# Two one-block passes in place of one two-block pass at the end of a first layer

## The chip, the core and the metric

The kernel runs on one core of one Trainium2 chip. The metric is the device time of one execution in microseconds (us). Its engines are named as in the profile: PE is TensorE's matmuls and PEld its weight loads, DVE is VectorE, ACT is ScalarE, POOL is GpSimd, SP is SyncE, whose queue issues the DMAs.

## The reference

Two branches read the same rows x (2048 rows of 512) and are mixed by a gate per row.

```python
g = sigmoid((x * gate_w).sum(-1, keepdims=True))

# a: attention over all 2048 rows, 32 heads of 16
q, k, v = split_heads(x @ wqkv)
p = softmax(q @ k.T * 16 ** -0.5)
a = merge_heads(p @ v) @ wo

# b: a token mixer, F = 1792
h = (x - mean) / sqrt(var + 1e-5)              # per row
u = einsum("bsd,sf->bdf", h, w1) + b1          # (1, 512, 1792)
u = gelu(u)                                    # tanh form
y = einsum("bdf,fs->bds", u, w2) + b2
b = transpose(y)                               # (1, 2048, 512)

out = g * a + (1 - g) * b
```

## The kernel before

Every product keeps float32 precision with three matmuls: each operand is split into a high and a low part (`split`: a rounding copy, then a subtraction), and the products high-high, high-low and low-high add up in PSUM.

The stages that follow one another on TensorE are the values v, the projections of keys and queries (`project`, L75), the mixer's first layer (`layer`, L424), and then 128 attention phases in which the second layer's matmuls (L1076), the remaining query projections and the output projection run beside the scores (L1067), on the other half of the array's rows.

**The first layer.** The output u has 14 blocks of 128 columns of F. A pass makes up to four blocks at once (`NB` = 512 columns), each in a PSUM bank of its own (`bank`), and goes through the 16 row blocks c of h. There are passes of 4, 4, 4 and 2 blocks. For each c, `weight()` issues the load of a coming piece of w1 (`load_weight`, L146, on SyncE's queue), splits the piece that is next in line (`split_weight`: the cast w_hi on ScalarE at L67, the subtraction w_lo on GpSimd at L68) and gives out the oldest one that is split. There are four raw buffers and three each of w_hi and w_lo, so a split runs as soon as TensorE is done with the piece three before it. A piece is 128 rows by 512 columns, in the last pass 128 by 256. The first layer's last pass begins with row block 8 and ends with 7, so that the second half of h is free halfway through it; the memory of that half goes to attention's tiles (ot, the second query stack and others). `load_next` issues small loads of the first key and query stacks at every other c.

**The gelu** of a block is a generator of seven steps on two engines in turn: add the bias (VectorE, L433, which frees the PSUM bank), square (ScalarE, L435), the cubic factor times u (VectorE, L437 and L438), tanh (ScalarE, L440), outer product (VectorE, L442), high part (ScalarE, L444), low part (VectorE, L446). Its tiles gu and gs have two buffers each. The gelus of a pass run in the next pass. In passes 1 and 2 (counted from 0) the compiler's scheduler places them. In pass 3 the queues of ScalarE, VectorE and GpSimd follow the written order (`manual_schedule`), and the four gelus of pass 2 take a step per row block, beginning at row blocks 0, 1, 7 and 8:

```python
for i, step in enumerate(gelus):
    if 0 <= at - i // 2 * STEPS - i % 2 < STEPS:
        next(step)
```

**The late blocks.** The two blocks of the last pass have their gelus in the first attention phases: `late_u` adds the bias at once (L549), which frees their banks for scores; then `squares` (L555), `cubic` (L559), `inner` (L563), `tanh` (L566), `outer` (L570) and `outer_parts` (the two parts) are called at points of phases 0 to 3 given by `amid` (before the last two scores of a phase), `later` (after the phase's exps) and `on_dve`. All but the tanh run on VectorE. They work in `late_s`, one of two large tiles into which `load_xt` (L597) later brings a piece of transposed x.

**An attention phase** makes 16 score tiles. Ten of them get their exp on ScalarE straight from PSUM, six singly (L1093) and four as two pairs (L1031); six are copied out by VectorE (L1089) and get one long exp together (L1102). In attention all five engines follow the written order. The scores of a phase use seven banks in turn.

Of the kernel before, what the change touches and what calls it, by code (L numbers as in the profile page):

```python
# [13 lines left out]
AF = mybir.ActivationFunctionType  # L14
ALU = mybir.AluOpType
# [8 lines left out]
P = 128  # L24
S = 2048
D = 512
F = 1792
H = 32
DH = 16
NS = S // P  # L30
ND = D // P
NF = F // P
NB = 512
# [4 lines left out]
GELU_A = 0.044715  # L38
# [22 lines left out]
def gated_mix(ctx: ExitStack, tc: tile.TileContext, a_x, a_wqkv, a_wo, b_w1, b_b1, b_w2, b_b2, gate_w, out):  # L61
    nc = tc.nc
# [30 lines left out]
    g = const.tile([P, NS], F32, name="g")  # L93
# [29 lines left out]
    xt_lo = xt_pool.tile([P, ND, S], F32R, name="xt_lo")  # L123


    order = {f0: [(c + (NS // 2 if f0 + NB >= F else 0)) % NS for c in range(NS)] for f0 in range(0, F, NB)}
    blocks = [b_w1[c * P : (c + 1) * P, f0 : min(f0 + NB, F)] for f0 in order for c in order[f0]]
    blocks += [
        b_w2[c * P : min(c + 4, NF) * P, t * P : (t + 1) * P].rearrange("(k p) s -> p k s", p=P)
        for t in range(NS)  # L130
# [26 lines left out]
    def weight():  # L157
        load_weight()
        split_weight()
        return ready.pop(0)  # L160
# [17 lines left out]
    with tc.tile_pool(name="vp", bufs=1, side="right") as pool:  # L178
# [122 lines left out]
        for t in range(2, NS):  # L301
# [9 lines left out]
            ps = bank()  # L311
# [22 lines left out]
    h_hi, h_lo = {}, {}  # L334
# [28 lines left out]
    if True:  # L363
# [19 lines left out]
        for b in range(ND):  # L383
            wk_b, wq_b = qk_w.pop(0), qk_w.pop(0)
            kmax = bd.tile([P, NQ], F32, name="kmax")
            for at, (n, keys) in enumerate(jobs):
                ps = project(wk_b if keys else wq_b, n)
# [11 lines left out]
                if at in (2, 5):  # L399
                    c = 2 * b + at // 3  # L400
# [16 lines left out]
    u_hi = u_pool.tile([P, NF, D], F32R, name="u_hi")  # L417
    u_lo = u_pool.tile([P, NF, D], F32R, name="u_lo")

    def layer(ps, hi, lo, rhs, first, last):  # L420
        for i, p in list(enumerate(ps))[:: 1 if len(ps) == NB // P else -1]:
            wh, wl = hi[:, i * P : (i + 1) * P], lo[:, i * P : (i + 1) * P]
            for k, (a, b) in enumerate(((wh, rhs[0]), (wh, rhs[1]), (wl, rhs[0]))):
                nc.tensor.matmul(p, a, b, start=first and k == 0, stop=last and k == 2)  # L424

    with tc.tile_pool(name="gl", bufs=2, side="right") as gl:

        def gelu(ps, fb):

            u = gl.tile([P, D], F32, name="gu")  # L430
            s = gl.tile([P, D], F32, name="gs")
            hi, lo = u_hi[:, fb, :], u_lo[:, fb, :]
            nc.vector.tensor_scalar_add(u, ps, b1[:, fb : fb + 1])  # L433
            yield
            nc.scalar.activation(s, u, AF.Square)  # L435
            yield
            nc.vector.tensor_scalar(s, s, GELU_A, 1.0, ALU.mult, ALU.add)  # L437
            nc.vector.tensor_mul(s, s, u)  # L438
            yield
            nc.scalar.activation(s, s, AF.Tanh, scale=GELU_C)  # L440
            yield
            nc.vector.scalar_tensor_tensor(u, s, 1.0, u, ALU.add, ALU.mult)  # L442
            yield
            nc.scalar.copy(hi, u)  # L444
            yield
            nc.vector.tensor_tensor(lo, u, hi.bitcast(F32), ALU.subtract)  # L446
            yield

        beside = {mybir.EngineType.Activation, mybir.EngineType.DVE, mybir.EngineType.Pool}
        for c in range(AHEAD):  # L450
            ln_load(NH + c)


        def shift_rows(engine, t):
            for i in range(2):
                engine.memset(t[i * HALF + SHIFT[0] : i * HALF + SHIFT[0] + DH].bitcast(F32), -1.0)

        landed, waiting = [], []

        def stack(dst, src, which, pair, planes):  # L460
            b, r0 = divmod(pair * 2 * DH, P)
            for i in range(2):
                rows = slice(r0 + i * DH, r0 + (i + 1) * DH)
                for row, *part in planes:
                    at = slice(i * HALF + row, i * HALF + row + DH)
                    waiting.append((dst[at].bitcast(F32), src[b][part[which], rows, :]))

        def load_next():
            if waiting:
                landed.append(nc.sync.dma_start(*waiting.pop(0)))  # L470

        def load_all():
            while waiting:
                load_next()

        def load_k(g):
            t = k_bufs[g % 2]
            stack(t, kp_d, 1, g % NP, PAIRS)
            if g:
                load_all()  # L480
            return t

        def load_q(g):
            half, pair = divmod(g, NP)
            t = q_bufs[g % 2]
            stack(t, qp_d[half], 0, pair, [*PAIRS, SHIFT])
            if g:
                load_all()
            return t

        k_bufs, q_bufs = [], []

        def first_loads():
            k_bufs.append(first_stacks.tile([P, S], F32R, name="ks"))
            q_bufs.append(first_stacks.tile([P, QW], F32R, name="qs"))
            shift_rows(nc.vector, k_bufs[0])
            return {0: load_k(0)}, {0: load_q(0)}

        STEPS = 7
        gelus = []  # L500
        for f0, cs in order.items():
            n = min(NB, F - f0) // P
            ps = [bank() for _ in range(n)]
            in_order = f0 == 0 or f0 + NB >= F
            if f0 == NB:
                kt, qt = first_loads()
            if not in_order:
                for step in gelus:
                    list(step)
                gelus = []  # L510
            with tc.manual_schedule(engines=beside) if in_order else ExitStack():
                for at, c in enumerate(cs):
                    hi, lo = weight()

                    if f0 == 0 and AHEAD < c <= NH:
                        ln_load(NH + c - 1)
                    if f0 == 0 and AHEAD < c <= NH + AHEAD:
                        ln_rows(NH + c - AHEAD - 1)
                    layer(ps, hi, lo, (h_hi[c], h_lo[c]), at == 0, at == NS - 1)
                    if at % 2:  # L520
                        load_next()
                    for i, step in enumerate(gelus):
                        if 0 <= at - i // 2 * STEPS - i % 2 < STEPS:
                            next(step)
            gelus = [gelu(ps[i], f0 // P + i) for i in range(n)]
    h_ctx.close()


# [17 lines left out]
    for i, p in reversed(list(enumerate(ps))):  # L546
        u = out_pool.tile([P, D], F32, name="row", bufs=3)
        at = NF - len(ps) + i
# [136 lines left out]
    calls, later, amid = {}, {}, {}  # L685
# [4 lines left out]
    def on_dve(at, *what):  # L690
        later.setdefault(at, []).append(what)
# [161 lines left out]
            on_dve(2 * at + 2, *finish)  # L853
        return put(steps, at, [len(steps)])

    for i in range(2):
        on_dve(1 + i, tanh, i)
        on_dve(2 + i, outer_parts, i)
    for p, mid, what, i in (
        (0, True, squares, 0),  # L860
        (0, False, cubic, 0),
        (1, True, inner, 0),
        (1, False, squares, 1),
        (1, False, cubic, 1),
        (2, True, inner, 1),
        (2, False, outer, 0),
        (3, True, outer, 1),
    ):
        if mid:
            amid.setdefault(p, []).append((what, i))  # L870
        else:
            later.setdefault(p, []).insert(1 if what is cubic and i else 0, (what, i))
    call(3, load_xt, 2)
    for b in range(ND):
        call(6 + b, nc.sync.dma_start, v_d[b], vb[b][:, :BV])
    at, queries = 0, [(b, n) for n in (2, 3) for b in range(ND)]
    for t in range(NS):
        at = put(second_layer(t), at, [14] * 3)
# [432 lines left out]
```

## Time and profile before

| | |
|---|---|
| median of 3 runs | 1265.53 us (1265.07 to 1266.18) |
| profiled execution | 1265.31 us, span 1263.5 us |
| granted TensorE clock | 0.999 |
| first layer (L424) | 122.9 to 277.6 us of the span |
| attention phases | from 277.5 us on |
| HBM read, written | 105.39 MB, 44.68 MB |

The page gives the busy time of each engine, the span in 40 slices, the DMA queues, the chain of work that ended last, and groups of instructions. Rows of a timeline are read as: start, duration (both us), engine, line, operation, tiles written and read, shapes, and in brackets how long the engine had idled and what released it; several instructions of one line in a row are merged (x2, x6), and their duration is then from the start of the first to the end of the last. A row of windows gives for each engine its busy time and, in brackets, its instructions, then the granted clock, the share of DMA time and GB/s. All times count from the start of the span.

### The profile page before, as it was taken

How to read it: one execution, taken by the hardware profiler on the slowest of the kernel's cores; microseconds unless marked ns; L12 is line 12 of the kernel's file. 1: busy time of each engine (PE TensorE's matmuls, PEld its weight loads, DVE VectorE, ACT ScalarE, POOL GpSimd, SP SyncE). 2: the span in 40 equal slices, each digit the busy share in tenths (PEclk: the TensorE clock that was granted, in tenths of full speed). 3: DMA queues.
4: the chain of work that ended last, by engine and by line, in shares of the span. 5: the costliest groups of instructions: out<-in, count | busy, mean ns of one | idle time of the engine just before them, and what ended most of it. 6: DMA issues, size and time to landing. Idle time of an engine off the chain costs nothing.

```text
span 1263.5 us, 32833 instructions
## 1 busy us (share of the span) xinstructions
PE 1254.8 (99%) x13342; PEld 829.2 (66%) x13342; DVE 856.7 (68%) x1562; ACT 1069.0 (85%) x1405; POOL 198.6 (16%) x316
## 2 busy tenths in 40 slices
PE   9999999999999999999999999999999999999998
PEld 7888888875666666666666666666666666666656
DVE  5675453178767676767677677776777677678883
ACT  4443343269999999999999999999999999999990
POOL 0220444461010101010110101111111111000000
PEclk9999999999999999999999999999999999999999
DMA  4799443244744444544344433444543443366611
GB/s 134 251 340 329 143 122 106 81 127 110 214 121 104 90 102 85 158 86 97 77 105 94 99 90 83 91 87 81 113 101 73 90 100 60 56 166 175 151 60 70
DMA packets 100556, 152.32 MB, mean 121 GB/s; under 512 B 17109, under 2 KB 56171, under 8 KB 96300
## 3 DMA queue, kind: packets, MB, share of 16 engines
q1 hardware_dynamic: 99820, 149.08, 46.0%
q8 instruction: 107, 1.75, 0.6%
q10 hardware_dynamic: 576, 1.05, 0.2%
q14 instruction: 53, 0.43, 0.1%
HBM read 105.39 MB, written 44.68 MB: 119 GB/s over the span
## 4 chain that ended last, share of the span: by engine, by line
PE 96%; DVE 2%; ACT 1%; issue 0%; DVEq 0%
PE av L963 31%; PE s L1067 21%; PE acc L424 12%; PE t L1067 9%; PE acc L75 8%; PE t L963 5%; PE dn L1076 3%; PE u L1067 3%; PE pa L1162 2%; DVE pe L1089 1%; PE acc L199 1%; PE acc L268 0%; DVE ot L985 0%; PE acc L245 0%; ACT p L1093 0%; ACT pe L1102 0%
## 5 line engine op out<-in xcount | busy, mean ns | idle before, releaser
L1093 ACT ACTIVATE p<-s 128x512 f32<-128x512 f32 x768 | 411.9, 789 | 0.1
L1102 ACT ACTIVATE pe<-pe 128x3072 f32<-128x3072 f32 x129 | 380.9, 2954 | 0.0
L1067 PE MATMUL s<-qs,ks 64*128 64x512 f32 x1280 | 329.8, 400 | 0.6 <-ACT p L1093 0.6
L1089 DVE COPY pe<-s 128x512 f32<-128x512 f32 x512 | 323.6, 685 | 5.5 <-PE s L1067 1.5
L1067 PEld LDWEIGHTS s<-qs,ks 64*128 64x128 f32 x1280 | 225.7, 184 | 92.7 <-issue 52.3
L1031 ACT ACTIVATE p<-t 128x1024 f32<-128x1024 f32 x256 | 278.7, 1267 | 0.0
L963 PE MATMUL av<-p,v 128*32 128x256 f32 x3880 | 227.2, 379 | 0.0
L1089 DVE COPY pe<-u 128x512 f32<-128x512 f32 x256 | 164.8, 685 | 67.1 <-PE u L1067 67.1
L963 PE MATMUL av<-pe,v 128*32 128x256 f32 x3072 | 192.5, 383 | 0.0
L985 DVE TENSOR_TENSOR ot<-av,ot 128x512 f32<-128x512 f32 (+2 forms) x160 | 93.0, 582 | 140.9 <-PE av L963 139.6
L68 POOL TENSOR_TENSOR w_lo<-w_raw,w_hi 128x512 fp32r<-128x512 f32 (+1 forms) x128 | 153.0, 1202 | 196.8 <-ACT w_hi L67 99.9
L1076 PE MATMUL dn<-u_lo,w_hi 64*128 64x512 f32 x448 | 181.0, 404 | 0.0
L1076 PE MATMUL dn<-u_hi,w_hi 64*128 64x512 f32 x448 | 180.7, 403 | 0.0
L963 PEld LDWEIGHTS av<-p,v 128*32 128x32 f32 x3880 | 126.0, 110 | 83.3 <-ACT p L1093 0.2
L1076 PE MATMUL dn<-u_hi,w_lo 64*128 64x512 f32 x448 | 180.6, 403 | 0.0
L1067 PE MATMUL t<-qs,ks 64*128 64x512 f32 x512 | 142.5, 413 | 0.0
L963 PEld LDWEIGHTS av<-pe,v 128*32 128x32 f32 x3072 | 86.8, 109 | 80.7 <-ACT p L1093 35.7
L1080 POOL MEMSET token<- 1x1 f32 x128 | 11.3, 88 | 742.7 <-PE dn L1076 679.4
L67 ACT CAST w_hi<-w_raw 128x512 fp32r<-128x512 f32 (+1 forms) x67 | 38.0, 569 | 82.7 <-PE acc L424 63.1
L1067 PEld LDWEIGHTS t<-qs,ks 64*128 64x128 f32 x512 | 73.2, 184 | 50.8 <-ACT p L1093 48.6
L424 PE MATMUL acc<-h_hi,w_hi 128*128 128x512 f32 x224 | 87.9, 392 | 0.0
L424 PE MATMUL acc<-h_hi,w_lo 128*128 128x512 f32 x224 | 87.9, 392 | 0.0
(171 smaller groups left out, 1615.8 us busy)
## 6 DMA issues: line engine op xcount, KB each, us to landing
w_raw<-in_B_w_dram SPq DMA_DIRECT2D x96, 256.0 KB
ks<-kp SPq DMA_DIRECT2D x192, 128.0 KB
qs<-qp SPq DMA_DIRECT2D x256, 64.0 KB
kp<-pc SPq DMA_DIRECT2D x16, 512.0 KB
qp<-pc SPq DMA_DIRECT2D x8, 768.0 KB
qp<-row SPq DMA_DIRECT2D x24, 256.0 KB
v<-v SPq DMA_DIRECT2D x4, 1088.0 KB
x<-in_A_x_dram SPq DMA_DIRECT2D x16, 256.0 KB
```

Source lines behind the costliest of these rows:

```text
L67: copy(hi, src)
L68: return sub(lo, src, hi.bitcast(F32), ALU.subtract)
L75: nc.tensor.matmul(ps, a, b, start=start and n == 0, stop=stop and n == last)
L424: nc.tensor.matmul(p, a, b, start=first and k == 0, stop=last and k == 2)
L963: mm = nc.tensor.matmul(av[32 * j : 32 * (j + 1), i * QC : (i + 1) * QC], vb[b][:, v_at : v_at + 32], pt[:, h * QC : (h + 1) * QC], start= ...
L985: latest["add"] = nc.vector.tensor_tensor(x, y, x, ALU.add)
L1031: pairs_done.append(nc.scalar.activation(pt, twos[low, low + 1], AF.Exp, scale=SCALE))
L1067: nc.tensor.matmul(s, kt[grp][rows_i, c * P : (c + 1) * P], qt[grp][rows_i, qb * NB : (qb + 1) * NB], start=True, stop=True,)
L1076: mm = nc.tensor.matmul(ps, a[half], b[half], start=begin and not second, stop=last and bool(second))
L1089: nc.vector.tensor_copy(pt, s)
L1093: one = nc.scalar.activation(pt, s, AF.Exp, scale=SCALE)
L1102: done = nc.scalar.activation(x, x, AF.Exp, scale=SCALE)
```

## The change

The last pass of two blocks becomes two passes of one block each, over the same rows in the same order (8 to 15, 0 to 7). Their weights come in pieces of four row blocks by 128 columns, so one piece of 128 by 512 lasts for four row blocks, 12 matmuls. `layer` gets an offset, n0, for the place of a row block in its piece.

Of the four gelus of the third pass, three run in the first of the two passes, beginning at row blocks 0, 5 and 9, and the fourth in the second, at 0; there the gelu of the first one-block pass begins at row block 4. One block is left as a late block, and the calls in the attention phases are written for it alone. In `gelu` the scale of the cubic term moves into the square on ScalarE, and one combined operation on VectorE takes the place of two.

```diff
-    order = {f0: [(c + (NS // 2 if f0 + NB >= F else 0)) % NS for c in range(NS)] for f0 in range(0, F, NB)}
-    blocks = [b_w1[c * P : (c + 1) * P, f0 : min(f0 + NB, F)] for f0 in order for c in order[f0]]
+    starts = [0, NB, 2 * NB, F - 2 * P, F - P, F]
+    order = {f0: [(c + (NS // 2 if f0 + NB >= F else 0)) % NS for c in range(NS)] for f0 in starts[:-1]}
+    width = {f0: f1 - f0 for f0, f1 in zip(starts, starts[1:])}
+    blocks = [b_w1[c * P : (c + 1) * P, f0 : f0 + NB] for f0 in order if width[f0] == NB for c in order[f0]]
+    blocks += [
+        b_w1[c * P : (c + 4) * P, f0 : f0 + P].rearrange("(k p) s -> p k s", p=P)
+        for f0 in order
+        if width[f0] == P
+        for c in order[f0][::4]
+    ]
...
-    def layer(ps, hi, lo, rhs, first, last):
-        for i, p in list(enumerate(ps))[:: 1 if len(ps) == NB // P else -1]:
+    def layer(ps, hi, lo, rhs, first, last, n0=0):
+        for i, p in enumerate(ps, n0):
...
-            nc.scalar.activation(s, u, AF.Square)
+            nc.scalar.activation(s, u, AF.Square, scale=GELU_A**0.5)
             yield
-            nc.vector.tensor_scalar(s, s, GELU_A, 1.0, ALU.mult, ALU.add)
-            nc.vector.tensor_mul(s, s, u)
+            nc.vector.scalar_tensor_tensor(s, s, 1.0, u, ALU.add, ALU.mult)
...
-            n = min(NB, F - f0) // P
+            n = width[f0] // P
...
-                    hi, lo = weight()
+                    if n > 1 or at % 4 == 0:
+                        hi, lo = weight()
...
-                    layer(ps, hi, lo, (h_hi[c], h_lo[c]), at == 0, at == NS - 1)
+                    layer(ps, hi, lo, (h_hi[c], h_lo[c]), at == 0, at == NS - 1, 0 if n > 1 else at % 4)
                     if at % 2:
                         load_next()
-                    for i, step in enumerate(gelus):
-                        if 0 <= at - i // 2 * STEPS - i % 2 < STEPS:
+                    for begin, step in gelus:
+                        if 0 <= at - begin < STEPS:
                             next(step)
-            gelus = [gelu(ps[i], f0 // P + i) for i in range(n)]
+            if f0 == F - 2 * P:
+                gelus = [(b - NS, g) for b, g in gelus if b >= NS] + [(4, gelu(ps[0], f0 // P))]
+                gelus.sort(key=lambda x: x[0])
+            else:
+                gelus = [(b, gelu(ps[i], f0 // P + i)) for i, b in zip(range(n), (0, 5, 9, NS))]
...
-    for i in range(2):
-        on_dve(1 + i, tanh, i)
-        on_dve(2 + i, outer_parts, i)
-    for p, mid, what, i in (
-        (0, True, squares, 0),
-        (0, False, cubic, 0),
-        (1, True, inner, 0),
-        (1, False, squares, 1),
-        (1, False, cubic, 1),
-        (2, True, inner, 1),
-        (2, False, outer, 0),
-        (3, True, outer, 1),
-    ):
...
+    amid[0] = [(squares, 0)]
+    on_dve(0, cubic, 0)
+    amid[1] = [(inner, 0)]
+    on_dve(1, tanh, 0)
+    on_dve(2, outer, 0)
+    on_dve(2, outer_parts, 0)
```

More of the change, by code (lines that the diff above doesn't have):

```diff
@@ L507, in gated_mix @@
             if not in_order:
-                for step in gelus:
+                for _, step in gelus:
                     list(step)
@@ L854, in put_whole @@
         return put(steps, at, [len(steps)])
-    for i in range(2):
-        on_dve(1 + i, tanh, i)
-        on_dve(2 + i, outer_parts, i)
-    for p, mid, what, i in (
-        (0, True, squares, 0),
-        (0, False, cubic, 0),
-        (1, True, inner, 0),
-        (1, False, squares, 1),
-        (1, False, cubic, 1),
-        (2, True, inner, 1),
-        (2, False, outer, 0),
-        (3, True, outer, 1),
-    ):
[L869 to L872, printed above, removed]
+    amid[0] = [(squares, 0)]
[4 more added lines that the diff above has]
+    on_dve(2, outer_parts, 0)
     call(3, load_xt, 2)
```

## The prediction

> **What bounds the kernel now.** I read the page first: busy shares, then the 40 slices, then the chain of waits around the first layer, then busy time by windows, and last the timeline of each engine from 253 us to 317 us, where the change sits.
>
> ```profile
> PE 1254.8 (99%) x13342; PEld 829.2 (66%) x13342; DVE 856.7 (68%) x1562; ACT 1069.0 (85%) x1405; POOL 198.6 (16%) x316
> ACT  4443343269999999999999999999999999999990
> 122.92 154.68 PE acc L424 x672
> 255.20:277.50 22.30, 22.30 (x98) 17.89 (x96) 15.05 (x19) 13.34 (x29) 14.63 (x17) 1.00 0.40 119
> L1093 ACT ACTIVATE p<-s 128x512 f32<-128x512 f32 x704 | 378.3, 795 | 0.0
> L1102 ACT ACTIVATE pe<-pe 128x3072 f32<-128x3072 f32 x118 | 351.7, 2980 | 0.0
> L1031 ACT ACTIVATE p<-t 128x1024 f32<-128x1024 f32 x234 | 255.4, 1273 | 0.0
> ```
>
> The first layer is one unbroken chain of 672 TensorE matmuls (third line), 0.230 us apart; its last pass, the window 255.2 to 277.5, has TensorE busy 22.30 of 22.30 us, VectorE 15.05, ScalarE 13.34, GpSimd 14.63. From there ScalarE takes over: its three kinds of exp between 330 and 1200 us have 0.0 us of idle time before them. So two things count: when ScalarE's stream of exps begins, and how much other ScalarE work lies inside it. Time is lost or won nowhere else unless TensorE stalls in the first layer.
>
> **What the change removes.** The period of the attention phases shows the price of a late tanh (L566):
>
> ```profile
> 290.29 2.93 ACT L1102 ACTIVATE pe<-pe 128x3072 f32<-128x3072 f32 x1
> 292.95 0.78 ACT L566 ACTIVATE big<-big 128x512 f32<-128x512 f32 x1
> 298.15 3.00 ACT L1102 ACTIVATE pe<-pe 128x3072 f32<-128x3072 f32 x1
> 300.82 0.84 ACT L566 ACTIVATE big<-big 128x512 f32<-128x512 f32 x1
> 306.08 3.00 ACT L1102 ACTIVATE pe<-pe 128x3072 f32<-128x3072 f32 x1
> 313.49 3.00 ACT L1102 ACTIVATE pe<-pe 128x3072 f32<-128x3072 f32 x1
> 320.91 3.00 ACT L1102 ACTIVATE pe<-pe 128x3072 f32<-128x3072 f32 x1
> ```
>
> From one long exp to the next it is 7.93 us where a tanh stands between (298.15 to 306.08), and 7.41 and 7.42 us where none does. One of the two tanhs goes: **minus 0.52 us**. The second block's six VectorE steps in phases 1 to 3 go too (square, cubic, inner, outer, high, low part), but VectorE is busy 68% and ScalarE never waits for it there: nothing. Its add after the first layer (L549) goes as well; that one belongs to the boundary, below.
>
> **What it moves without a price.** TensorE issues the same 96 matmuls in the last passes, with the same weights, so 22.3 us stay. Sixteen loads, ScalarE casts and GpSimd subtractions of 128x256 become eight of 128x512, paced at one per 12 matmuls as in the three wide passes. A load of 256 KB is wanted every 2.76 us:
>
> ```profile
> 234.00:236.80 2.80, 2.80 (x14) 2.25 (x13) 0.00 (x0) 0.62 (x1) 1.30 (x2) 1.00 0.32 97
> SPq L146 <- POOL w_lo L68: 59.8, 33, 4.2
> 304.57 0.83 SPq L597 DMA_DIRECT2D big<-xt  x2
> 266.74 0.53 POOL L999 MEMSET ot<- 128x512 f32 x1 [0.40 <-PE acc L424]
> ```
>
> A wide pass moves 97 GB/s at a DMA share of 0.32, and SyncE's queue waits for free buffers (second row), not TensorE for data. Shorter runs (512 B for 2 KB) may double that share to 0.64, still under one, so I cost the loads at nothing; the cover is the four raw buffers, about three groups of 2.76 us, and a load slower than that would stall TensorE by the excess. On SyncE the next group's query rows wait for the second half of h, which is now free a quarter of the two passes later, about 5.5 us; they are used four phases on. The reload of xt (L597), which at 304.57 had waited for the second late block's outer step, starts one phase earlier; nobody waits for it before phase 6. GpSimd's clearing of ot moves back with h: no one waits.
>
> The gelu loses one VectorE operation: a scale (0.54 us, the row at 259.09 below) and a multiply (0.69 at 259.66) become one combined operation. In the first three passes that is hidden under TensorE.
>
> **What it adds: a chain of gelu steps.** Before, four gelus lie beside the 22.3 us, two at a time; now five lie there: three staggered in the first pass, two in the second. Two details of the order set the cost. First, each weight split on ScalarE waits until TensorE has finished a whole group, since there are three w_hi buffers:
>
> ```profile
> 255.32 0.39 PE L424 MATMUL acc<-h_hi,w_hi 128*128 128x512 f32 x1
> 256.72 0.41 ACT L67 CAST w_hi<-w_raw 128x256 fp32r<-128x256 f32 x1 [0.99 <-PE acc L424]
> 258.44 0.63 ACT L435 ACTIVATE gs<-gu 128x512 f32<-128x512 f32 x1
> 259.09 0.54 DVE L437 TENSOR_SCALAR gs<-gs 128x512 f32<-128x512 f32 x1 [4.23 <-ACT gs L435]
> 259.66 0.69 DVE L438 TENSOR_TENSOR gs<-gs,gu 128x512 f32<-128x512 f32 x1
> 275.26 0.61 ACT L444 CAST u_hi<-gu 128x512 fp32r<-128x512 f32 x1
> 275.90 1.37 DVE L446 TENSOR_TENSOR u_lo<-gu,u_hi 128x512 fp32r<-128x512 f32 x1 [0.71 <-ACT u_hi L444]
> ```
>
> A group was six matmuls (255.32 to 256.72); it becomes twelve, so the first split can run only at 255.32 + 2.76 = 258.08, and every ScalarE step written behind it in the queue waits with it: the first square starts about 258.6, after the split's 0.54 (what one ScalarE operation of this size takes in a row of them: 3.26 by six at 278.06, below). Second, the steps of one gelu alternate between ScalarE and VectorE, and in VectorE's queue the next gelu's add stands behind the outer step of the one before. What one step costs:
>
> ```profile
> 221.30 1.48 DVE L442 SCALAR_TENSOR_TENSOR gu<-gs,gu 128x512 f32<-128x512 f32 x2
> 261.90 1.21 DVE L442 SCALAR_TENSOR_TENSOR gu<-gs,gu 128x512 f32<-128x512 f32 x1
> 272.98 1.06 DVE L442 SCALAR_TENSOR_TENSOR gu<-gs,gu 128x512 f32<-128x512 f32 x1
> 215.16 0.68 DVE L446 TENSOR_TENSOR u_lo<-gu,u_hi 128x512 fp32r<-128x512 f32 x1
> 253.41 1.45 DVE L433 TENSOR_SCALAR gu<-acc,b 128x512 f32<-128x512 f32 x2 [27.22 <-PE acc L424]
> 272.49 1.00 POOL L68 TENSOR_TENSOR w_lo<-w_raw,w_hi 128x256 fp32r<-128x256 f32 x1
> 236.42 1.29 POOL L68 TENSOR_TENSOR w_lo<-w_raw,w_hi 128x512 fp32r<-128x512 f32 x1 [1.50 <-ACT w_hi L67]
> 275.43 4.24 POOL L68 TENSOR_TENSOR w_lo<-w_raw,w_hi 128x512 fp32r<-128x512 f32 x3 [0.79 <-ACT w_hi L67]
> ```
>
> ScalarE steps are 0.63, 0.63 and 0.62. A combined VectorE step is 0.74 alone (the 1.48 is two) and 1.06 to 1.21 where GpSimd subtracts at the same time (272.49 to 273.49 beside 272.98). GpSimd will subtract eight times 1.29 us, under half of the 22.3, so I take 0.85, nearer to the undisturbed row; for the closing subtraction 0.75 (0.68 alone), for the add 0.75 (1.45 is two, overlapped by a little). A hand-over I estimate at 0.05 from the rows (258.44 + 0.63 to 259.09, 0.02; 275.26 + 0.61 to 275.90, 0.03), rounded up.
>
> From one gelu's square to the next one's: 0.63 + 0.85 + 0.63 + 0.85 + 0.75 + 5 x 0.05 = 3.96. From a square to the gelu's end: 0.63 + 0.85 + 0.63 + 0.85 + 0.62 + 0.75 + 0.25 = 4.58. In the written order: squares at 258.6, 262.5, 266.5; the third gelu ends at 271.1, and the second pass begins with an add (0.80 with its hand-over), square at 271.9, the fifth gelu's square at 275.9, its end at 280.45. TensorE ends at 277.6. So the chain outlasts the pass.
>
> Who waits for that is seen at the boundary:
>
> ```profile
> 277.19 1.40 DVE L549 TENSOR_SCALAR row<-acc,b 128x512 f32<-128x512 f32 x2
> 277.21 0.39 PE L424 MATMUL acc<-h_hi,w_lo 128*128 128x512 f32 x1
> 277.99 0.50 PE L1067 MATMUL s<-qs,ks 64*128 64x512 f32 x1
> 278.06 3.26 ACT L1093 ACTIVATE p<-s 128x512 f32<-128x512 f32 x6
> 278.52 2.52 DVE L1089 COPY pe<-s 128x512 f32<-128x512 f32 x4
> 281.56 1.28 DVE L1089 COPY pe<-u 128x512 f32<-128x512 f32 x2
> 282.96 2.84 ACT L1102 ACTIVATE pe<-pe 128x3072 f32<-128x3072 f32 x1
> ```
>
> The second score matmul, at 277.99, starts 0.05 after the first late add ended (277.19 + 0.75 = 277.94): it takes that block's bank. Behind it on TensorE stand all other scores, behind these ScalarE's exps and VectorE's copies, whose last pair ends at 282.84 with the long exp at 282.96. There is no slack. With a late add at 280.45 + 0.05 + 0.75 = 281.25, the stream begins 281.25 - 277.94 = 3.3 us late; with the tanh gone, **plus 2.8**. That is the written order in full. But engines' queues need not follow it across two stages: the clearing of ot at 266.74 belongs to attention and ran in the middle of the last pass. If the second pass's first gelu overlaps the third one like the others, 271.9 becomes 270.5 and the late add ends at 279.8: 1.85 late, **plus 1.3**. I take the middle, **plus 2.1**. On the profiled execution's 1265.31 that gives 1267.4; the median of the runs is 0.22 higher, 1265.53, so 1267.6 for a median. A measurement of this kernel can tell about 0.2% from no change, 2.53 us, so the line is at 1268.06.
>
> **Rivals.** *Absorbed.* Total work is no obstacle: with five gelus ScalarE has 23 operations of 0.54 = 12.4 us in 22.3. If steps run when ready, the fifth gelu ends about with TensorE. Then the late add runs at 277.65 to 278.40, 0.46 late, or behind one last subtraction of 0.68, 1.14 late: net -0.06 to +0.62, 1265.5 to 1266.2. For it speaks the row at 266.74; against it, that within the last pass ScalarE's split and gelu rows follow strictly in turn.
>
> *GpSimd slows every VectorE step (slower).* The place is the same chain: twelve VectorE steps with two inputs. At 1.1 us each instead of 0.85 and 0.75, spacing is 4.46 and the rest 5.43; the late add ends at 284.4 in written order, 6.5 late, net +6.0, 1271.5. It decides from a mean of about 0.95, where even the overlapped order passes 2.53. For it: the 1.37 at 275.90, beside the first of three subtractions of 128x512 that ran on to 279.67; against it: subtractions fill under half of the time. The Trainium skill, "SBUF — State Buffer", Who interferes with whom, says the two engines share a port as an exclusive lock and the loser waits for the whole instruction; by that a caught step would cost up to 1.29 more, and with half of the twelve caught the chain some 7.7, an estimate. Of that rule the rows here show only a part: 1.06 for 0.74 beside 0.51 us of overlap.
>
> *Only the tanh counts.* If chain and late add fit as well as now, -0.52: 1265.0. It needs the fifth gelu to be done before TensorE ends. More cannot be won, since neither TensorE's 672 matmuls nor any other exp goes.
>
> **How the numbers follow.** Forecast 0.47, of which 0.10 lies over the line of 2.53; absorbed 0.20; slower by GpSimd 0.25; tanh only 0.08, of which 0.03 for a gain that I have overlooked. Slower: 0.25 + 0.10 = 0.35; within: 0.37 + 0.20 + 0.05 = 0.62; faster: 0.03. The range runs from 1264.9, under the tanh case, to 1269.6, which takes in all of the forecast's span and the slower rival up to about +4.1, a mean VectorE step of about 1.0; what lies beyond, some 0.15, is left out.
>
> **What would show it.** Phase 3's period should be 7.41 in place of 7.93, with one L566 tanh. The last passes should keep TensorE busy throughout; a gap there refutes the free loads. The first split should start near 258.1 and the first square near 258.6. The last low part of a gelu should end after TensorE's last L424 matmul, and the one late add at 279.8 to 281.3, with the second score just behind it; an add at 278.4 means absorbed, one past 282 means the slow VectorE steps, and then their mean must be over 0.95. The prediction is wrong if the time moves while the late add does not, or if the exps behind it show idle time.

## The result, and the profile after

| | before | after |
|---|---|---|
| median (20 runs each) | 1265.57 us (1265.02 to 1267.68) | 1267.74 us (1266.87 to 1270.12) |
| profiled execution | 1265.31 us | 1267.72 us |
| span of that execution | 1263.5 us | 1265.8 us |

The ratio is 1.0017, with a 95% interval of 1.001 to 1.0023: slower by about 2.2 us, inside what the prediction calls no change.

The prediction's number, 1267.6, is close, but the trace does not give it for the reasons of the prediction. The lines of after.py are 7 to 12 higher than before's around the first layer and 1 higher in attention: the layer is L432; a gelu is the add L441, square L443, cubic step L445, tanh L447, outer product L449, high part L451, low part L453; the late add is L561, the late tanh L578, a single exp L1094, the long exp L1103, VectorE's copies L1090, scores L1068.

The page first: its busy times, ScalarE in the 40 slices, and the group of the score matmuls with the idle time ahead of it.

```profile
PE 1256.3 (99%) x13342; PEld 829.9 (66%) x13342; DVE 846.1 (67%) x1547; ACT 1068.8 (84%) x1399; POOL 194.2 (15%) x308
ACT  4443344259999999999999999999999999999990
L1068 PE MATMUL s<-qs,ks 64*128 64x512 f32 x1280 | 329.4, 400 | 2.2 <-DVE row L561 2.2
```

TensorE has the same 13342 matmuls as before, but it has gained one wait of 2.2 us, on the late add. Windows of the last two passes, of the stretch in which that wait ends, and of the two behind it (PE, PEld, DVE, ACT and POOL busy, then granted clock, DMA share, GB/s):

```profile
255.20:277.50 22.30, 22.30 (x98) 17.98 (x96) 14.44 (x17) 11.88 (x20) 9.53 (x8) 1.00 0.33 95
279.99:283.40 3.41, 1.88 (x12) 0.94 (x13) 3.30 (x6) 2.92 (x7) 1.63 (x2) 1.00 0.64 168
283.40:286.81 3.41, 3.41 (x28) 1.78 (x30) 2.81 (x5) 2.56 (x4) 2.02 (x3) 0.50 1.07 142
286.81:290.22 3.41, 3.41 (x46) 2.10 (x38) 1.84 (x5) 3.41 (x4) 1.86 (x1) 1.00 0.56 75
```

The passes themselves are as good as before: TensorE 22.30 of 22.30. What is new lies behind them: in the third row the granted clock is 0.50.

The chain of gelus, first on ScalarE (the first split and the five squares), then on VectorE (the groups of its steps with two inputs, with the mean ns of one; then single rows, and among them the GpSimd subtraction that the step at 268.47 ran into), then the score that waits on TensorE:

```profile
258.21 0.62 ACT L67 CAST w_hi<-w_raw 128x512 fp32r<-128x512 f32 x1 [2.18 <-PE acc L432]
258.74 0.63 ACT L443 ACTIVATE gs<-gu 128x512 f32<-128x512 f32 x1
262.84 0.64 ACT L443 ACTIVATE gs<-gu 128x512 f32<-128x512 f32 x1
267.07 0.63 ACT L443 ACTIVATE gs<-gu 128x512 f32<-128x512 f32 x1
272.09 0.63 ACT L443 ACTIVATE gs<-gu 128x512 f32<-128x512 f32 x1
275.98 0.63 ACT L443 ACTIVATE gs<-gu 128x512 f32<-128x512 f32 x1
```

```profile
L445 DVE SCALAR_TENSOR_TENSOR gs<-gs,gu 128x512 f32<-128x512 f32 x5 | 5.1, 1012 | 5.1 <-ACT gs L443 5.1
L453 DVE TENSOR_TENSOR u_lo<-gu,u_hi 128x512 fp32r<-128x512 f32 x5 | 4.8, 951 | 1.4 <-ACT u_hi L451 1.4
L449 DVE SCALAR_TENSOR_TENSOR gu<-gs,gu 128x512 f32<-128x512 f32 x5 | 3.9, 785 | 3.5 <-ACT gs L447 3.5
```

```profile
267.80 0.75 DVE L441 TENSOR_SCALAR gu<-acc,b 128x512 f32<-128x512 f32 x1
268.29 1.30 POOL L68 TENSOR_TENSOR w_lo<-w_raw,w_hi 128x512 fp32r<-128x512 f32 x1 [2.52 <-ACT w_hi L67]
268.47 1.67 DVE L445 SCALAR_TENSOR_TENSOR gs<-gs,gu 128x512 f32<-128x512 f32 x1
276.86 0.68 DVE L445 SCALAR_TENSOR_TENSOR gs<-gs,gu 128x512 f32<-128x512 f32 x1
279.61 0.99 DVE L453 TENSOR_TENSOR u_lo<-gu,u_hi 128x512 fp32r<-128x512 f32 x1 [0.69 <-ACT u_hi L451]
280.71 0.75 DVE L561 TENSOR_SCALAR row<-acc,b 128x512 f32<-128x512 f32 x1
281.38 2.47 DVE L1090 COPY pe<-s 128x512 f32<-128x512 f32 x4
285.06 1.29 DVE L1090 COPY pe<-u 128x512 f32<-128x512 f32 x2 [0.60 <-PE u L1068]
```

```profile
278.92 0.39 PE L1068 MATMUL s<-qs,ks 64*128 64x512 f32 x1
281.52 0.50 PE L1068 MATMUL s<-qs,ks 64*128 64x512 f32 x1 [2.21 <-DVE row L561]
```

The squares stand one behind the other, 3.9 to 5.0 us apart: each waits until the gelu before has come to its high part, so no two gelus fill each other's gaps, and the last low part ends at 280.60, 2.9 us after TensorE's last first-layer matmul. The late add follows at once and ends at 281.46. Six scores have run before; the **seventh** waits for the bank.

The stream of exps (the long exp of the first phase with the idle time ahead of it, the one late tanh, the next long exps):

```profile
286.45 2.77 ACT L1103 ACTIVATE pe<-pe 128x3072 f32<-128x3072 f32 x1 [0.79 <-DVE pe L1090]
296.44 0.69 ACT L578 ACTIVATE big<-big 128x512 f32<-128x512 f32 x1
301.63 2.92 ACT L1103 ACTIVATE pe<-pe 128x3072 f32<-128x3072 f32 x1
308.96 3.02 ACT L1103 ACTIVATE pe<-pe 128x3072 f32<-128x3072 f32 x1
```

Against before's 282.96, 298.15 and 306.08, the long exp is 3.49 us late, 3.48 late, and after the phase whose tanh went 2.88 late (its period is 7.33 for 7.93). The lag then stays. The last VectorE operation of the program, in before and then in after, each with the span from its page:

```profile
span 1263.5 us, 32833 instructions
1257.33 0.75 DVE L1205 SCALAR_TENSOR_TENSOR base<-pa,g,base 128x512 f32<-128x512 f32 x1 [2.03 <-PE pa L1162]
```

```profile
span 1265.8 us, 32773 instructions
1260.36 0.75 DVE L1206 SCALAR_TENSOR_TENSOR base<-pa,g,base 128x512 f32<-128x512 f32 x1 [2.03 <-PE pa L1163]
```

It comes 3.03 us late, but the span is only 2.3 longer: from the start of this operation to the end it is 6.2 us in before and 5.4 in after. So the account of the two traces is 3.49 - 0.60 + 0.15 (small shifts on the way) - 0.75 = 2.3. Three questions follow: why the late add is late, what the stream's lag consists of, and why the end is shorter.

### The profile page after: what moved, and what is told of

The parts are those of the page before. It is cut to its first block, busy times and chain, and to the rows that moved or that the text cites. A ratio compares the mean times of both kernels' runs of the same rounds, so it can differ in the third digit from the quotient of the medians.

```text
span 1265.8 us, 32773 instructions
## 1 busy us (share of the span) xinstructions
PE 1256.3 (99%) x13342; PEld 829.9 (66%) x13342; DVE 846.1 (67%) x1547; ACT 1068.8 (84%) x1399; POOL 194.2 (15%) x308
## 4 chain that ended last, share of the span: by engine, by line
PE 96%; DVE 3%; ACT 1%; issue 0%; DVEq 0%; ACTq 0%
PE av L964 32%; PE s L1068 21%; PE acc L432 11%; PE t L1068 9%; PE acc L75 8%; PE t L964 5%; PE dn L1077 4%; PE u L1068 3%; PE pa L1163 2%; DVE pe L1090 1%; PE acc L207 1%; PE acc L276 1%; DVE gs L445 0%; DVE u_lo L453 0%; DVE ot L986 0%; DVE gu L449 0%
## 5 line engine op out<-in xcount | busy, mean ns | idle before, releaser
L1094 ACT ACTIVATE p<-s 128x512 f32<-128x512 f32 x768 | 412.0, 790 | 0.5 <-PE dn L1077 0.5
L1103 ACT ACTIVATE pe<-pe 128x3072 f32<-128x3072 f32 x129 | 381.0, 2955 | 1.0 <-DVE pe L1090 0.8
L1068 PE MATMUL s<-qs,ks 64*128 64x512 f32 x1280 | 329.4, 400 | 2.2 <-DVE row L561 2.2
L1090 DVE COPY pe<-s 128x512 f32<-128x512 f32 x512 | 323.5, 686 | 4.5 <-PE dn L1077 1.1
L1068 PEld LDWEIGHTS s<-qs,ks 64*128 64x128 f32 x1280 | 225.6, 184 | 93.1 <-issue 52.3
L1090 DVE COPY pe<-u 128x512 f32<-128x512 f32 x256 | 164.9, 686 | 68.5 <-PE u L1068 68.5
L68 POOL TENSOR_TENSOR w_lo<-w_raw,w_hi 128x512 fp32r<-128x512 f32 x120 | 148.6, 1244 | 202.5 <-ACT w_hi L67 104.1
L1068 PE MATMUL t<-qs,ks 64*128 64x512 f32 x512 | 143.2, 414 | 0.0
L1068 PEld LDWEIGHTS t<-qs,ks 64*128 64x128 f32 x512 | 73.2, 185 | 51.4 <-ACT p L1094 50.1
L67 ACT CAST w_hi<-w_raw 128x512 fp32r<-128x512 f32 x59 | 36.4, 619 | 78.6 <-PE acc L432 63.1
L432 PE MATMUL acc<-h_hi,w_hi 128*128 128x512 f32 x224 | 87.9, 393 | 0.0
L432 PE MATMUL acc<-h_hi,w_lo 128*128 128x512 f32 x224 | 87.9, 392 | 0.0
```

Source lines behind the costliest of these rows:

```text
L67: copy(hi, src)
L68: return sub(lo, src, hi.bitcast(F32), ALU.subtract)
L1068: nc.tensor.matmul(s, kt[grp][rows_i, c * P : (c + 1) * P], qt[grp][rows_i, qb * NB : (qb + 1) * NB], start=True, stop=True,)
L1090: nc.vector.tensor_copy(pt, s)
L1094: one = nc.scalar.activation(pt, s, AF.Exp, scale=SCALE)
L1103: done = nc.scalar.activation(x, x, AF.Exp, scale=SCALE)
```

## The experiments

Each was timed in five rounds against the kernel before on the same chip. Medians of before in these comparisons lie between 1265.55 and 1265.76, so a difference between two variants from different comparisons is uncertain by about 0.2 us.

**Two gelus at a time again.** The kernel after with its gelus begun in pairs, and nothing else changed.

```diff
-                gelus = ... + [(4, gelu(ps[0], f0 // P))]
+                gelus = ... + [(1, gelu(ps[0], f0 // P))]
...
-                gelus = [... zip(range(n), (0, 5, 9, NS))]
+                gelus = [... zip(range(n), (0, 1, 7, 8))]
```

> The changed kernel with other starting points for the gelus alone: the third pass's four in pairs in the first one-block pass (row blocks 0, 1, 7, 8, as before the change), the fifth at row block 1 of the second. Chain theory: two gelus fill each other's gaps, all four end soon after the first one-block pass and the fifth about 3 us before TensorE ends, so the late add runs at 277.7 to 278.5, no score waits for it, and the kernel takes the price of one tanh less than before: 1265.57 - 0.5 = about 1265.1. Rival (the two passes themselves, their pieces of four row blocks or the short runs of their loads cost the time): it stays near the changed kernel, 1267.7. Rival (VectorE is simply short of time): the same VectorE work in the same window, late add near 280, 1267 or more.

Measured 1264.15 us, ratio 0.9988 (0.9979 to 0.9997): 3.6 us less than after, and 0.9 less than expected, most of it at the end of the span (below). Its late add and first long exp, and the groups of its VectorE steps between 259 and 281 us:

```profile
278.35 0.75 DVE L561 TENSOR_SCALAR row<-acc,b 128x512 f32<-128x512 f32 x1
283.40 2.77 ACT L1103 ACTIVATE pe<-pe 128x3072 f32<-128x3072 f32 x1
```

```profile
L453 DVE TENSOR_TENSOR u_lo<-gu,u_hi 128x512 fp32r<-128x512 f32 x5 | 5.1, 1041 | 1.1 <-ACT u_hi L451 1.0
L449 DVE SCALAR_TENSOR_TENSOR gu<-gs,gu 128x512 f32<-128x512 f32 x5 | 4.4, 887 | 1.2 <-ACT gs L447 1.1
L445 DVE SCALAR_TENSOR_TENSOR gs<-gs,gu 128x512 f32<-128x512 f32 x5 | 4.0, 823 | 5.3 <-ACT gs L443 5.2
```

The add is 2.36 us earlier and TensorE has no wait. VectorE's steps are not faster: their mean is 0.92 us (1041, 887 and 823 ns) here and 0.92 in after (1012, 951 and 785 ns). What differs is that two gelus fill each other's hand-overs. The staggered order of the change costs the time, not the late block or its weights.

**GpSimd's reads away.** In the two one-block passes GpSimd clears w_lo (0.53 us) in place of the subtraction (1.29 us); the low parts of these weights are left out.

```diff
...
+    def cleared(lo, src, hi, op):
+        return nc.gpsimd.memset(lo.bitcast(F32), 0.0)
...
-                        hi, lo = weight()
+                        hi, lo = weight(cleared if n == 1 else None)
```

> The changed kernel, with GpSimd's eight subtractions in the two one-block passes replaced by clearing the low part (GpSimd then reads nothing from SBUF; the low parts of eight weight pieces are left out). Contention as the larger half of the lag: the seven VectorE steps that took 1.02 to 1.67 us beside GpSimd go to about 0.69, 3.4 us shorter in all, the chain ends near TensorE's end, late add at 277.7 to 278.4, time about 1265.1. Rival (the written order alone makes the lag, with VectorE steps at 0.69 to 0.75): by spacing 3.64 and rest 4.17 the late add would still end about 279.5 to 280, time about 1266.2. Rival (neither): 1267.7.

Measured 1264.59 us, ratio 0.9992 (0.9983 to 1.0001). The three groups of VectorE steps and the late add:

```profile
L456 DVE TENSOR_TENSOR u_lo<-gu,u_hi 128x512 fp32r<-128x512 f32 x5 | 3.5, 693 | 1.5 <-ACT u_hi L454 1.4
L452 DVE SCALAR_TENSOR_TENSOR gu<-gs,gu 128x512 f32<-128x512 f32 x5 | 3.5, 692 | 4.2 <-ACT gs L450 4.2
L448 DVE SCALAR_TENSOR_TENSOR gs<-gs,gu 128x512 f32<-128x512 f32 x5 | 3.4, 689 | 5.2 <-ACT gs L446 5.1
278.00 0.75 DVE L564 TENSOR_SCALAR row<-acc,b 128x512 f32<-128x512 f32 x1
```

Every step is now 0.69 us, and the same staggered order fits: the add is 2.71 us earlier than in after. So the late add has two causes that only together do harm: steps slowed by GpSimd (0.92 us for 0.69), and an order with no second gelu to hide it. Taking away either is enough.

**One VectorE operation more per gelu.** The kernel after with before's gelu formula.

```diff
-            nc.scalar.activation(s, u, AF.Square, scale=GELU_A**0.5)
+            nc.scalar.activation(s, u, AF.Square)
...
-            nc.vector.scalar_tensor_tensor(s, s, 1.0, u, ALU.add, ALU.mult)
+            nc.vector.tensor_scalar(s, s, GELU_A, 1.0, ALU.mult, ALU.add)
+            nc.vector.tensor_mul(s, s, u)
```

> The changed kernel with the old gelu: scale and multiply as two VectorE operations in place of one combined operation, nothing else. Chain theory: every one of the five gelus gets about 0.45 us longer between its square and its tanh, and all five stand in the chain: the late add moves from 280.7 to about 283, time 1267.74 + 2.2 = about 1269.9. Rival (the late add is held by TensorE's end and its bank, and the chain has slack): no change, 1267.7.

Measured 1271.74 us, ratio 1.0051 (1.0037 to 1.0065). The late add, the score that waits for it, the first long exp, and windows before and during a lowered clock:

```profile
283.16 0.75 DVE L562 TENSOR_SCALAR row<-acc,b 128x512 f32<-128x512 f32 x1
283.96 0.79 PE L1069 MATMUL s<-qs,ks 64*128 64x512 f32 x1 [4.34 <-DVE row L562]
289.59 2.77 ACT L1104 ACTIVATE pe<-pe 128x3072 f32<-128x3072 f32 x1 [0.72 <-DVE pe L1091]
278.04:281.45 3.41, 1.58 (x10) 0.88 (x10) 2.61 (x4) 1.76 (x4) 0.55 (x2) 1.00 0.57 164
281.45:288.28 6.83, 4.32 (x22) 2.97 (x26) 4.90 (x8) 5.50 (x10) 2.99 (x4) 0.50 0.76 139
```

The add is 2.45 us later than in after, the long exp 3.14, the time 4.0. So the chain is on the path, but the stream loses more than the add does: 0.7 us with the doubled half-clock stretch (6.83 us for 3.41), and another 0.8 at the end of the span (below).

**TensorE kept busy in the wait.** Two float32 products of zeros ahead of the seventh score of the first phase.

```diff
...
+                if p == 0 and n == 6:
+                    for _ in range(2):
+                        nc.tensor.matmul(
+                            beside[0][0], ident, small[:, :1].broadcast_to([P, NB]), start=False, stop=False
+                        )
```

> The changed kernel with two full-size float32 matmuls of a zero column, which add zero to the second layer's bank, ahead of the seventh score: TensorE works through its 2.2 us of waiting. In the changed kernel the granted clock is half from 283.4 to 286.8, two microseconds after that wait. Theory A (the wait alone counts; ScalarE and VectorE pace the phase): late add at 280.7 as before, time 1267.7, at most 0.2 less. Theory B (the half clock after the wait adds to the loss): the clock stays at 1.0, the first phase's last scores come about 0.5 us sooner, long exp at 285.7 to 286.0 in place of 286.45, time 1267.0 to 1267.3.

Measured 1266.83 us, ratio 1.001 (1.0001 to 1.0019): 0.9 us less than after. The added matmuls, the late add, the first long exp, and the windows that stand beside after's second and third:

```profile
278.92 1.99 PE L1047 MATMUL dn<-pad,ident 128*128 128x512 f32 x4
280.41 0.75 DVE L562 TENSOR_SCALAR row<-acc,b 128x512 f32<-128x512 f32 x1
285.45 2.77 ACT L1109 ACTIVATE pe<-pe 128x3072 f32<-128x3072 f32 x1 [0.27 <-DVE pe L1096]
279.99:283.40 3.41, 3.10 (x17) 1.34 (x17) 3.30 (x6) 2.91 (x7) 1.44 (x1) 1.00 0.80 188
283.40:286.81 3.41, 3.41 (x50) 2.01 (x48) 3.00 (x6) 3.14 (x3) 2.82 (x3) 1.00 0.97 127
```

The clock stays at 1.00. In this execution the add is 0.30 us earlier too, so the measure is the interval from the add's end to the long exp: 4.29 us here (281.16 to 285.45), 4.30 with the pairs (279.10 to 283.40) and without GpSimd's reads (278.75 to 283.05), 4.99 in after (281.46 to 286.45), 5.68 with the longer gelu (283.91 to 289.59). One half-clock stretch of 3.41 us costs the stream 0.7 us. Most of it is a wait of VectorE: in after its last two copies of the phase idled 0.60 us for scores that ran at half clock (the row at 285.06), and here they run without a wait.

**Another step behind the late add.** In before the interval is 5.02 us from the first late add's end (277.94), at full clock. Before has a second late add there, which ends at 278.59. Here the pairs kernel gets one more VectorE step behind its late add, which leaves its values as they are.

```diff
         nc.vector.tensor_scalar_add(u, p, b1[:, at : at + 1])
+        nc.vector.scalar_tensor_tensor(u, u, 0.0, u, ALU.add, ALU.max)
```

> The kernel with the pairs of gelus, and behind the one late add one more VectorE step of 128x512 that leaves its values as they are (about 0.69 us); it holds no bank of PSUM. Theory A (at the boundary the stream of exps is set by VectorE's order: late adds, then copies, then the long exp): the first long exp begins 0.65 to 0.7 us later behind the late add than in the kernel with the pairs (4.30 us behind the add's end), and the median goes from 1264.15 to 1264.8. Theory B (as the prediction had it, the scores on TensorE wait for the late add's bank and everything follows from them): the step holds nobody up, 1264.15 within 0.2.

Measured 1264.87 us, ratio 0.9994 (0.9985 to 1.0003), 0.7 more than the pairs.

```profile
278.46 0.83 DVE L562 SCALAR_TENSOR_TENSOR row<-row 128x512 f32<-128x512 f32 x1
283.59 2.77 ACT L1104 ACTIVATE pe<-pe 128x3072 f32<-128x3072 f32 x1 [0.28 <-DVE pe L1091]
```

The interval from the add's end (278.42) grows from 4.30 to 5.17, by the step and its hand-over. No score waits for this step, so at full clock the stream is set by VectorE's order at the boundary, add, copies, long exp, and not by TensorE's wait for a bank. A late block less there is worth 0.65 us.

**One tanh less in before.** The second block's late tanh is left out.

```diff
-        on_dve(1 + i, tanh, i)
+        if i == 0:
+            on_dve(1 + i, tanh, i)
```

> The kernel before, with the second late block's tanh left out (its other steps stay). If ScalarE is the bound throughout attention: 0.52 us less, 1265.05, and from one long exp to the next 7.41 us in the phase that took 7.93. Rival (TensorE takes the time back): 7.41 in that phase, but the lead over the kernel before is gone some phases on, 1265.57.

Measured 1265.23 us, ratio 0.9999 (0.999 to 1.0008). The long exps of phases 2 and 3:

```profile
297.93 3.00 ACT L1103 ACTIVATE pe<-pe 128x3072 f32<-128x3072 f32 x1
305.35 3.01 ACT L1103 ACTIVATE pe<-pe 128x3072 f32<-128x3072 f32 x1
```

The period falls from 7.93 to 7.42, as the prediction had it, and the last operation on base comes 0.60 us earlier. The median is only 0.3 under that of before in the same comparison, and its interval takes in no change. In the profiled execution 6.6 us follow at the end in place of 6.2; why is not shown.

**The end of the span.** Three kernels change the length of VectorE's instruction stream where nothing waits for it: the pairs and the kernel after with 15 one-element clears in the third pass, and before with the change's shorter gelu alone.

```diff
...
+            if f0 == 2 * NB:
+                for i in range(15):
+                    nc.vector.memset(small[:1, i : i + 1], 0.0)
```

> The version with the gelus in pairs, plus fifteen one-element memsets on VectorE in the third pass, where VectorE is idle for 27 us: nothing on the path changes, but VectorE's program has about as many instructions as before the change. In the kernel before, and in both variants with as many VectorE instructions, VectorE comes to the last barrier about 0.8 us after the other engines, with one more instruction fetch on its queue after the last matmul (8 for 7). Theory (the length of VectorE's program decides that fetch): last matmul where it was, the end 0.8 us later, 1264.15 + 0.8 = about 1264.95. Rival (that 0.8 us goes with the gelus' places or with chance): no change, 1264.15.

> The kernel before, with the one-operation-shorter gelu of the change alone (twelve VectorE instructions fewer, all beside TensorE's matmuls). Theory (what hides under TensorE costs nothing): last matmul at 1256.9 as before, to 0.2. If twelve fewer instructions are enough to save the last fetch, the end comes 0.8 us earlier, 1264.75; else 1265.55. Rival (the shorter gelu is itself worth something in the first layer): last matmul earlier by over 0.5 us.

> The kernel after, with 15 one-element clears added to VectorE's queue in the third pass of the first layer, where TensorE covers them; VectorE then has 1562 counted instructions, as the kernel before has, in place of 1547. Theory A (the kernel after ends 0.8 us sooner behind its last matmul because VectorE's instruction stream is shorter, and that hid part of its loss): the stretch from the last addition to base to the end of the span grows from 5.4 us to 6.2-6.6, and the median by 0.8 to 1.1, 1268.5 to 1268.85, with the late add where it was (281.46). Theory B (the end of the span has nothing to do with it; the 0.8 us are an accident of that execution): no change, 1267.74 within 0.3.

The padded pairs measured 1265.12 us, ratio 0.9996 (0.9986 to 1.0005); before with the shorter gelu 1264.52, 0.9993 (0.9984 to 1.0002); the padded after 1268.63, 1.0022 (1.0013 to 1.0031). So 15 clears of one element cost 0.97 and 0.89 us, although TensorE covers them (0.84 and 0.70 with each variant counted against before in its own comparison; the runs of the padded after spread from 1267.46 to 1269.83). The shorter gelu, which the first layer hides, gains 1.2 (0.8 between the two profiled executions, 0.6 of it at the end of the span). The page's count of VectorE instructions sorts all kernels by the time from the start of the last operation on base to the end of the span:

| kernel | VectorE instructions | us to the end of the span |
|---|---|---|
| before; one tanh less; padded pairs; padded after | 1562 each | 6.2; 6.6; 6.6; 6.8 |
| after with the longer gelu | 1560 | 6.3 |
| before with the shorter gelu | 1550 | 5.6 |
| kept busy in the wait; pairs with a second step | 1548 each | 5.3; 5.2 |
| after; pairs; earlier pairs; without GpSimd's reads | 1547 each | 5.4; 5.5; 5.3; 5.4 |

The two groups do not overlap. In the trace of before VectorE's event at the last barrier comes 6.29 us after the start of the last matmul, about 1 us after those of the other engines (5.17 to 5.31); in after it comes at 5.28, with them (5.14 to 5.28). On the instruction queue q14 eight fetches lie behind the last matmul in all five kernels of the first two rows, and seven in all the others. That the program needs one more fetch from some length on, between 1550 and 1560 counted instructions, fits all of this; that the fetch is what VectorE waits for there was not tried by itself.

**Earlier pairs.** Since the pairs' late add is at 278.35, 0.4 us after TensorE's last first-layer matmul ends (277.96), the second pair and the fifth gelu were begun a row block earlier.

```diff
-                gelus = [... zip(range(n), (0, 1, 7, 8))]
+                gelus = [... zip(range(n), (0, 1, 6, 7))]
...
-                gelus = ... + [(1, gelu(ps[0], f0 // P))]
+                gelus = ... + [(0, gelu(ps[0], f0 // P))]
```

> The version with pairs, with the second pair a row block earlier (0, 1, 6, 7) and the fifth gelu at row block 0 of the second pass in place of 1. In the version with pairs the fifth gelu's last step ended at 278.24, just ahead of the late add at 278.35 (0.45 us after TensorE's end). Chain theory: the late add can come at most 0.45 us sooner, time 1263.7 to 1264.15. If the order on VectorE gets worse instead, it goes up by as much as the late add slips.

Measured 1263.72 us (1263.57 to 1264.02), ratio 0.9985 (0.9976 to 0.9994): the fastest of all, 2.0 us under before and 4.0 under after.

```profile
277.91 0.75 DVE L561 TENSOR_SCALAR row<-acc,b 128x512 f32<-128x512 f32 x1
282.94 2.84 ACT L1103 ACTIVATE pe<-pe 128x3072 f32<-128x3072 f32 x1
```

The first long exp is where before has it (282.96), and with 0.5 of the tanh and 0.9 at the end of the span gained, that makes 1.4 of the 2.0, which is also what the two profiled executions differ by.

## Why the prediction was right or wrong

**Right: nothing is lost in the passes.** The eight loads of the two passes cost nothing (DMA share 0.33, not the 0.64 allowed for, and TensorE 22.30 of 22.30), the first split and first square came at 258.21 and 258.74 (258.08 and 258.6 predicted), and the tanh was worth 0.51 to 0.60 (0.52).

**Right in kind: the late add is late because the chain of gelus outlasts TensorE.** The run without GpSimd's reads and the pairs both remove the wait and 3.2 to 3.6 us with it.

**Wrong: "I take the middle".** The written order gave 281.25, the overlapped one 279.8; the trace shows the written order almost to the tenth (squares at 258.7, 262.8, 267.1, 272.1 and 276.0 against 258.6, 262.5, 266.5, 271.9 and 275.9) and an add that ends at 281.46. Only the bias add of the second pass's first gelu slipped ahead (267.80), and its square still waited behind the third gelu's high part. That the written order fits so closely is partly luck: with its add done early, the fourth square came 5.0 us after the third and not 5.4, while the slowed steps cost more than was put for them. The reason given for the middle, that a clearing of ot ran early, was evidence for GpSimd's queue and said nothing on ScalarE's.

**Wrong size: the VectorE step.** 0.85 and 0.75 became a mean of 0.92. The slow rival had the right mechanism at less than its size: its threshold, a mean of 0.95 in the order of after, was not reached, and in another order even 0.96 fits (the earlier pairs: 1254, 823 and 803 ns in the same three groups). The rule of the Trainium skill, "SBUF — State Buffer", Who interferes with whom, that GpSimd and VectorE lock each other out of a shared port, agrees as to who interferes: without GpSimd's reading subtractions no step is slowed. It agrees as to how much, too. Seven of the 15 steps began while a subtraction was running, and each of them ended 0.55 us after that subtraction's end (the one at 268.47 at 270.14, the subtraction at 269.59); the other eight took 0.68 or 0.69. So a caught step lost what was left of the subtraction, 0.30 to 0.98 us and 3.4 in all, never the whole 1.29. The prediction's own row of 1.06 in before fits this (an end at 274.04, 0.55 behind 273.49), so the rows then at hand could have given the size.

**Wrong: "The second score matmul" and "no slack".** The bank of the one late block is wanted by the seventh score, and the stream hangs on VectorE's copies behind the late adds. Counted from the second add of before (278.59) the lag is 0.65 us less than the prediction's count from the first (277.94). That gain was overlooked.

**Overlooked: TensorE's clock.** The wait of 2.2 us left TensorE busy 1.88 of 3.41 us, and in the next 3.41 us the granted clock was 0.50, which cost 0.7. The stretch before, from 276.57 to 279.99 with TensorE busy 2.74 of 3.42 us (80%), had left it at 1.00. The Trainium skill, "TensorE: Matmul & The Clock Gate", Part 1, has a half-rate state after an idle window of about 3.4 us. The length agrees with the trace (3.41, and 6.83 after the longer wait); the condition does not: here the stretch before was 55% busy, in the kernel with the longer gelu 46% (1.58 of 3.41), and neither was idle throughout.

**Overlooked: the end of the span.** The shorter gelu took 12 instructions off VectorE's count, the whole change 15, and with them went about 0.8 us of the end. The prediction costed this part at nothing because TensorE covers it.

Put together: the add 3.52 late, minus 0.65, plus 0.7, is about the 3.5 by which the long exp is late, where the prediction had 2.6; minus 0.60 for the tanh; minus 0.75 at the end. The term for the late stream was 0.9 too small and the end 0.75 too large, and the two nearly cancelled: that the forecast of 1267.6 met 1267.74 so closely is luck. The padded after, 1268.63, is about what the change costs without the shorter end: 1.0 over the forecast and over the prediction's own line of 1268.06, and 2.9 over before in its own comparison, beyond the 2.53 of that line.

## What to carry to other kernels

A chain that alternates between two engines should run two at a time wherever a deadline follows: at the same cost per step, pairs ended 2.4 us before the staggered order. Where a boundary has several waits, look for the one that the bounding engine's next operation really hangs on (here copies in VectorE's queue, not the matmul that waits for a bank), and ask what an idle stretch does to TensorE's clock afterwards. When differences of a microsecond matter, compare the end of the span separately, since it can move by 0.8 us with the mere number of instructions.

## What the runs showed of the hardware

- The granted clock of TensorE went to 0.50 for 3.41 us after a stretch of 3.41 us in which TensorE had been busy 55%, and for 6.83 us after one with 46%, in a wait of 4.34 us; after a stretch with 80% it stayed at 1.00. Two products of zeros, 1.99 us, in the wait kept it at 1.00.
- A gelu step of VectorE with two inputs of 128x512 that began while GpSimd subtracted (1.29 us for 128x512) ended 0.55 us after the subtraction's end, in all 12 such cases of after's 39 steps and all 15 of before's 36; the other steps took 0.68 or 0.69 us. With clears by GpSimd in place of subtractions all 15 took 0.68 or 0.69. The bias adds out of PSUM stayed at 0.75 in both.
- The end of the span was 5.2 to 5.6 us with up to 1550 VectorE instructions and 6.2 to 6.8 with 1560 or more.
